# Block 2's spectrum by row number mod 4, its filter turned by transfers, and two product sums of block 3 by accumulating transfers, in a convolution and SwiGLU kernel

## The chip, the cores and the metric

One Trainium2 chip, one of its cores. The metric is the device time of one execution in microseconds (us), from the run before the change: 261.34 us, the median of three runs (261.23 to 261.5). Engines are called as the profile calls them: PE (TensorE, matmuls), PEld (its weight loads), DVE (VectorE), ACT (ScalarE), POOL (GpSimd) and SP (SyncE, which here only issues transfers). Each engine works through its own instructions in the order in which the program issues them.

## The reference

```python
x = A_q                                   # 2048 x 640, bf16
n = layernorm(x)
k_shift = causal 4-tap convolution of A_k, per channel (A_shift_k)
kv = k_shift * A_v
y  = causal long convolution of kv with A_ssm_k, per channel (by FFT of length 2 * 2048)
y  = y + kv * A_ssm_D
h  = x + n * y
u  = layernorm(h)
out = h + (silu(u @ w_gate) * (u @ w_up)) @ w_down     # 640 -> 1728 -> 640
```

(This is the reference in short, not its text.) The long convolution is what the change touches: each output row depends on all earlier rows of kv.

## The kernel before

**Tiles.** The 2048 rows are cut into four blocks of 512 (`BLK`). Within a block, row n lies on partition n // 4 as its row r = n mod 4, so a block is a tile of 128 partitions x 4 rows x 640 channels, 640 KB in bf16. Block j's output is the sum over i of the kv of block i convolved with pieces j - i and j - i - 1 of the filter. Each product is made in a spectrum of 512 odd frequencies, computed as matmuls with constant cosines and sines (`WF`; back with `WI`). A spectrum is a tile "S" of 128 x 2 x 4 x 640: two halves, each with two cosine and two sine rows of 640 channels, 1.25 MB.

**Stages of block j**, in the names that the program gives them: `g` turns the piece of the filter so that time lies on partitions; `G` is its spectrum; `h` (function `window`, or `window_of` in block 3) makes from G of this and the previous piece what is multiplied; `k` makes kv; `X` is kv's spectrum; `m0` to `mj` are the products X[i] * H[j-i] added up (`mac`); `n` is layernorm's statistics of x; `i` is the inverse with gate and addition of x; `t` normalises and turns h; `f` is the block's feed-forward part. The feed-forward part of block j-1 is written among the convolution stages of block j, so PE always has one of the two to do; that of block 3 (`f3`) comes alone at the end.

**The spectrum** (`transform`, from L381). "sub", the plain way, makes for each of four groups c of frequencies the sum of rows 0 and 2 (evicted doubled), then that of all rows (evicted as half 0): 32 matmuls of 128 x 320 columns and 8 evictions (L364 on ACT or L367 on DVE); half 1 is one DVE subtraction (L410). "four" uses a symmetry between rows of the same parity: for the even and the odd rows apart it makes two rows of sums and two of doubled parts, 16 matmuls and 8 evictions in all; DVE makes the rest by two `diffs` (L439, half a tile each), then 'hi4' (L443) for half 1 and 'lo4' for half 0. If the name is in `ADDLO`, which lists 'X2' already, lo4 is not a DVE instruction but an accumulating transfer (`add_into`, L278): POOL issues a DMA which adds a 640 KB tile into another one in SBUF. Before the change only X3, G3 and the inverses i2 and i3 go by four.

**The filter turned** (`g_turned`, L452). Normally, for each r, PE transposes five 128 x 128 pieces into PSUM (L471) and ACT or DVE evicts them (L473). A block in `GTURN` has instead one ACT copy of the whole tile into the order of rows (L457) and four DMA transposes of 160 KB, issued by SP (L461).

**The products** (`mac`, L703). After the first product of a block, each further one is four pairs on DVE: a product into a scratch tile (L746) and an addition or subtraction into the sum A (L747). For a pair listed in `ADDP` DVE makes the product alone (L741), and an accumulating transfer adds it (as for m11 before).

**The inverse** (`inverse`, L810): DVE first makes the difference and sum of the halves (L823, L826; the sum of block 2 by an accumulating transfer, `ADDINV`), then in "four" blocks the even rows' part (L843) and the odd rows' part (L858); PE makes row r from them (L878), DVE gates it (L892) and x is added (L905 or a transfer of POOL). The new h is normalised (L804 on DVE, L807 on ACT) and turned by PE (L926, evicted in L928) in block 0, and by DMA in the others.

**The feed-forward part**: groups of 256 columns; weights of a group are two loads of 320 KB (L959, issued by SP or POOL) into one slot of "big"; matmuls in L1022, evicted by ACT (L1014 with silu, L1012 plain), multiplied by DVE (L1016), then the down projection (L1110). Blocks 0 to 2 send their output by an accumulating transfer of POOL (L1117).

**What sets the order.** All instructions are first recorded as operations with their engine, tiles and dependencies (class `Plan`), and issued in an order written out by hand, the list `ORDER`. A negative number there stands for the operation's other engine: an eviction goes to DVE and not to ACT, a load to POOL's queue and not to SP's. Tiles take slots from small pools when their first operation comes in that order (12 of 640 KB called "big", 8 called "S", 5 rows, 4 pairs of PSUM banks) and give them back after their last; what comes next in a slot waits for it.

Of the kernel before, what the change touches and what calls it, by code (L numbers as in the profile page):

```python
# [41 lines left out]
LN1DVE = ()  # L42
LN2POOL = (1, 2)
HTURN = (1, 3, 2)
GTURN = (3,)
KTURN = (1, 2, 3)
SUM = {'X3': 'four', 'i2': 'four', 'i3': 'four', 'G3': 'four'}
ADDP = {(1, 1): ((0, 1),)}
ADDINV = (2,)
WHOLE3 = False  # L50
WARMUP = (18, 16, 16)
# [17 lines left out]
TW = PAD + BLK  # L69
CUTS = ("X0", "G0", "m", "i")  # L70
ORDER = [
# [36 lines left out]
SLOTS = {'S': 8, 'big': 12, 'kT': 0, 'tT': 1, 'row': 5, 'sg': 0, 'co': 2, 'ps': 4, 'sm': 6}  # L108
HOME = {t: "big" for t in ("scr", "x", "ld", "t4", "hT", "wgu", "diag")} | {"o": "row", "ps_c": "ps", "ps_f": "ps"}
SPLIT = ((0,), (1,))  # L110
# [102 lines left out]
def kernel(ctx: ExitStack, tc: tile.TileContext, A_q, A_k, A_v, A_shift_k, A_ssm_k, A_ssm_D, B_x,  # L213
# [19 lines left out]
    def new(tag):  # L233
        return Buf(HOME.get(tag, tag), None, tag)
# [26 lines left out]
    def dve(ns, fn, r, w, holds=()):  # L261
        return plan.add("dve", ns, fn, r, w, holds)
# [82 lines left out]
    def bits(halves=(0, 1), cs=(0, 1, 2, 3), ws=(0, 1)):  # L345

        return frozenset((h, c, w) for h in halves for c in cs for w in ws)
# [31 lines left out]
    def wide(n, ws):  # L379
        return n if len(ws) == 2 else n // 2 + 75  # L380
# [10 lines left out]
    def transform(src, dst, pieces, minus=None, name=None):  # L391

        how = SUM.get(name, "sub")
        for ws in pieces:
# [58 lines left out]
    def g_turned(g, drow=None):  # L453
        gT = new("t4")
        if plan.block in GTURN:
            by_r = new("scr")
# [356 lines left out]
    def inverse(A, x, n1, pieces=((0, 1),), minus=None, groups=(ROWS,)):  # L813
# [4 lines left out]
        for ws in pieces:  # L818
            if not minus:
# [10 lines left out]
                else:  # L830
                    dve(wide(1490, ws), low, [], [(A, bits(ws=ws))])
            four = not minus and SUM.get(f"i{plan.block}") == "four"
            if four:
# [404 lines left out]
    for j in range(1, NB):  # L1238
        def stage(name, j=j):
            plan.line(j, f"{name}{j}")  # L1240
# [23 lines left out]
        if last:  # L1264
            A = H[j]
            stage("m0")
            mac(A, X[0], H[j], True, at=(j, 0), adds=ADDP.get((j, 0), ()))
        stage("k")
# [4 lines left out]
        if not last:  # L1273
            stage("m0")
            A = Spec(new("S"))
            mac(A, X[0], H[j], True, at=(j, 0), adds=ADDP.get((j, 0), ()))
        for i in range(1, j + 1):
# [5 lines left out]
            else:  # L1283
                mac(A, X[i], H[j - i], False, adds=ADDP.get((j, i), ()), at=(j, i))
        stage("n")
# [45 lines left out]
```

## Time and profile before

| | |
|---|---|
| median of three runs | 261.34 us |
| the profiled execution | 261.3 us |
| its span | 259.6 us |
| granted clock of PE | 1.0 |
| PE busy | 251.3 us, 97% |
| DVE busy | 198.6 us, 77% |
| ACT busy | 180.0 us, 69% |
| POOL busy | 97.0 us, 37% |
| moved by DMA | 45.38 MB, 175 GB/s on average |

How to read it: the profile's page has numbered parts. The first gives the busy time of each engine, the second the same in 40 equal slices, a digit being tenths. Part 4 follows the chain of work that ended last back from the end. Part 5 groups instructions by line, engine, operation and tile: busy time, the mean of one, then the idle time before them with what ended it ("<- engine tile line"). Part 6 lists transfers with the median time from issue to landing. Beside the page there are views of the trace: the waits of one engine, its timeline with start, duration and idle time in brackets, and tables of busy time by stretch. In a timeline row "x4" is four instructions in a row that are shown as one. Matmuls are pipelined and their ends are modelled, so one is best priced from the start of a row to the start of the next. "Landing" counts from the issue of a transfer to its arrival. A busy share over the whole span mixes stages that have different limits; the stage shows which wait ends last there.

### The profile page before, as it was taken

To read this page: it belongs to the slowest core of one execution; us is meant where nothing else is said; L and a number is where in the kernel's file an instruction comes from. 1 tells how busy PE (TensorE), PEld (TensorE's weight loads), DVE (VectorE), ACT (ScalarE), POOL (GpSimd) and SP (SyncE) were. 2 spreads that over 40 slices of the span, in tenths; PEclk is the share of its full clock that TensorE was granted. 3 is DMA by queue.
4 is the path that set the end of the run, shared out by engine and by line. 5 is a ranking of instruction groups with operands and counts; after the bars stand their busy time and mean duration, and the time that the engine had idled before them with its cause. 6 is when DMAs were issued, how large, how long until landed. Compare 5 with 4: busy or idle time off the path is not lost.

```text
span 259.6 us, 4700 instructions
## 1 busy us (share of the span) xinstructions
PE 251.3 (97%) x1803; PEld 154.2 (59%) x1818; DVE 198.6 (77%) x259; ACT 180.0 (69%) x297; POOL 97.0 (37%) x115
## 2 busy tenths in 40 slices
PE   8999899999998999999999999999999999999994
PEld 7967577654654477754465477544456764444663
DVE  4679999999998999999999999999998200004403
ACT  2899999999998998569855985655497134637200
POOL 7961300008914199926117962240951022000000
PEclk9999999999999999999999999999999999999999
DMA  6997999979999998999997965994498546000002
GB/s 218 403 251 119 289 252 340 280 115 279 247 238 168 182 217 204 190 191 201 214 231 110 299 151 107 198 238 130 100 215 255 101 77 70 8 0 0 13 15 76
DMA packets 64752, 45.38 MB, mean 175 GB/s; under 512 B 31014, under 2 KB 60267, under 8 KB 64731
## 3 DMA queue, kind: packets, MB, share of 16 engines
q1 hardware_dynamic: 58896, 32.96, 51.1%
q0 software_dynamic: 5824, 12.13, 24.9%
q8 instruction: 14, 0.23, 0.4%
q14 instruction: 8, 0.06, 0.1%
q10 hardware_dynamic: 10, 0.01, 0.0%
HBM read 30.01 MB, written 4.59 MB: 133 GB/s over the span
## 4 chain that ended last, share of the span: by engine, by line
PE 78%; ACT 9%; DMA 6%; DVE 2%; issue 2%; SPq 1%; ACTq 0%; DVEq 0%
PE ps L1022 40%; PE ps L1110 23%; PE ps L375 10%; DMA big<-in_B_w_up_dram 4%; PE ps L878 3%; DMA big<-in_A_q_dram 3%; ACT T L565 2%; ACT big L364 1%; ACT S L364 1%; PE ps L648 1%; ACT row L757 1%; ACT big L664 1%; ACT big L473 1%; ACT tT L1014 1%; DVE row L892 1%
## 5 line engine op out<-in xcount | busy, mean ns | idle before, releaser
L1022 PE MATMUL ps<-big,big 128*128 128x512 bf16 x525 | 119.9, 379 | 1.7 <-DMA big<-in_B_w_up_dram 0.8
L1022 PEld LDWEIGHTS <-big 128*128 128x128 bf16 x540 | 52.5, 98 | 61.1 <-DMA big<-in_B_w_up_dram 1.3
L1110 PE MATMUL ps<-wd,tT 128*128 128x320 bf16 (+1 forms) x416 | 60.3, 299 | 0.0
L1110 PEld LDWEIGHTS <-tT 128*128 128x128 bf16 x416 | 40.7, 98 | 16.3
L1016 DVE TENSOR_TENSOR tT<-tT,co 128x2048 bf16<-128x2048 bf16 x12 | 14.5, 1219 | 34.4 <-ACT tT L1014 32.4
L375 PE MATMUL ps<-big,WF 128*128 128x320 bf16 x240 | 39.1, 299 | 1.3 <-ACT big L364 1.0
L1012 ACT CAST co<-ps 128x1024 bf16<-128x1024 f32 x24 | 24.2, 1011 | 17.3 <-PE ps L1022 16.8
L747 DVE TENSOR_TENSOR S<-S,big 128x2560 bf16<-128x2560 bf16 x23 | 34.3, 1492 | 1.2 <-DMA S<-big 0.5
L746 DVE TENSOR_TENSOR big<-S,S 128x2560 bf16<-128x2560 bf16 x23 | 34.1, 1485 | 0.2
L375 PEld LDWEIGHTS <-WF 128*128 128x128 bf16 x240 | 23.1, 97 | 12.8 <-issue 2.3
L1014 ACT ACTIVATE tT<-ps 128x1024 bf16<-128x1024 f32 x24 | 24.5, 1029 | 8.8 <-PE ps L1022 8.7
L757 ACT ACTIVATE row<-big 128x640 bf16<-128x640 bf16 x32 | 23.5, 742 | 1.8 <-DMA big<-in_A_q_dram 1.1
L807 ACT ACTIVATE row<-big,sm 128x640 bf16<-128x640 bf16 x23 | 20.3, 922 | 3.8 <-POOL sm L789 2.8
L1117 POOL DMA_DIRECT2D out_dram<-row x12 | 11.8, 1010 | 29.2 <-ACT row L1116 29.1
L364 ACT CAST S<-ps 128x320 bf16<-128x320 f32 (+1 forms) x36 | 19.4, 583 | 0.3
L1116 ACT CAST row<-ps 128x640 bf16<-128x640 f32 x12 | 8.1, 691 | 14.2 <-PE ps L1110 13.2
L364 ACT ACTIVATE big<-ps 128x640 bf16<-128x640 f32 (+1 forms) x24 | 15.6, 696 | 0.7 <-PE ps L375 0.7
L278 POOL DMA_DIRECT2D big<-row x8 | 7.0, 919 | 22.9 <-DVE row L892 22.9
L892 DVE SCALAR_TENSOR_TENSOR row<-row,ps 128x640 bf16<-128x640 bf16 x16 | 12.8, 815 | 1.1 <-PE ps L878 0.9
L278 POOL DMA_DIRECT2D S<-big x2 | 2.5, 1266 | 26.3 <-DVE S L719 19.1
L719 DVE TENSOR_TENSOR big<-S,S 128x2560 bf16<-128x2560 bf16 (+1 forms) x10 | 12.2, 1218 | 0.1
L959 POOL DMA_DIRECT2D big<-in_B_w_gate_dram x8 | 9.1, 1137 | 8.1 <-PE ps L1022 7.8
(110 smaller groups left out, 330.4 us busy)
## 6 DMA issues: line engine op xcount, KB each, us to landing
big<-in_B_w_up_dram SPq DMA_DIRECT2D x17, 320.0 KB, 5.1
big<-in_B_w_gate_dram SPq DMA_DIRECT2D x16, 320.0 KB, 4.7
big<-in_A_ssm_k_dram SPq DMA_DIRECT2D x4, 640.0 KB, 9.2
big<-in_A_q_dram SPq DMA_DIRECT2D x4, 640.0 KB, 7.6
big<-in_A_v_dram SPq DMA_DIRECT2D x4, 640.0 KB, 6.9
big<-in_B_w_gate_dram POOLq DMA_DIRECT2D x8, 320.0 KB, 7.2
big<-in_B_w_up_dram POOLq DMA_DIRECT2D x7, 320.0 KB, 6.7
wd<-in_B_w_down_dram SPq DMA_DIRECT2D x1, 2080.0 KB, 12.2
```

The costliest lines, as they stand in the source:

```text
L364: (lambda: nc.scalar.activation(dst(), src(), ACT.Copy, scale=2.0)) if twice else (lambda: nc.scalar.copy(dst(), src())),
L375: nc.tensor.matmul(ap(ps)[:, h, 0:NH], w, ap(src)[:, r, h * NH:(h + 1) * NH], start=(first and i == 0), stop=(last and i == len(rs) - 1), ...
L746: nc.vector.tensor_mul(flat2(b), X.part(xs), H.part(hs))
L747: f(A.part(dst), A.part(dst), flat2(b))
L757: act(825, lambda r=r, junk=junk: nc.scalar.activation(ap(junk), ap(x)[:, r, :], ACT.Square, scale=D ** -0.5, accum_out=sm(s, 1)[:, r:r + ...
L807: nc.scalar.activation(ap(row), ap(x)[:, r, :], ACT.Identity, bias=sm(s, 5)[:, r:r + 1], scale=sm(s, 4)[:, r:r + 1])
L892: nc.vector.scalar_tensor_tensor(two(ap(t)), two(ap(t)), 1.0, half(ap(ps)), op0=ALU.mult, op1=ALU.mult, accum_out=sm(s, 0)[:, r:r + 1])
L1012: act(1010, lambda ps=ps: nc.scalar.copy(ap(co)[:, at:at + 2, :], ap(ps)), src, [(co, gi % 2)])
L1014: act(1010, lambda ps=ps: nc.scalar.activation(ap(tT)[:, c:c + 2, :], ap(ps), ACT.Silu), src, [done(range(c, c + 2), ROWS)])
L1016: dve(1220, lambda: nc.vector.tensor_mul(ap(tT)[:, c - 2:c + 2, :], ap(tT)[:, c - 2:c + 2, :], ap(co)), [co], [done(range(c - 2, c + 2), R ...
L1022: nc.tensor.matmul(ap(ps)[:, i, :], ap(w)[:, k, off:off + P], ap(hT)[:, k, :], start=(k == 0), stop=(k == KT - 1))
L1110: nc.tensor.matmul(ap(ps)[:, hf, to:to + n], t, ap(wd)[:, c, col + (hf - hs[0]) * NH:col + (hf - hs[0]) * NH + n], start=(c == order[0]), ...
```

## The change

Four parts, all by settings and by the order:

- X2 is made the way of four (16 matmuls, two `diffs`, 'hi4', and 'lo4' by an accumulating transfer since 'X2' is in `ADDLO`).
- Block 2's g is turned by a copy of ACT and four DMA transposes.
- In block 3 the sum of X1's first product (the pair (0, 1) of m13) and the same one of m23 are added by accumulating transfers.
- The order is a new one. Besides the new operations it moves evictions between ACT and DVE, weight loads between POOL and SP (POOL issues 17 where it issued 20) and loads in the first 50 us; POOL has three accumulating transfers more and SP four transposes.

```diff
-GTURN = (3,)
+GTURN = (2, 3)
 KTURN = (1, 2, 3)
-SUM = {'X3': 'four', 'i2': 'four', 'i3': 'four', 'G3': 'four'}
-ADDP = {(1, 1): ((0, 1),)}
+SUM = {'X3': 'four', 'i2': 'four', 'i3': 'four', 'G3': 'four', 'X2': 'four'}
+ADDP = {(1, 1): ((0, 1),), (3, 1): ((0, 1),), (3, 2): ((0, 1),)}
...
 ORDER = [
-    0, 2, 31, 1, 4, 5, 7, 10, 6, 8, 16, 13, 12, 11, 22, 29, 26, 37, 27, 14, 3, 15, 23, 28, 42, -39, 9, 35, -37, 24, 39, 205, 40,
...
+    4, 0, 1, 42, 2, 31, 3, 16, 5, 7, 9, 6, 10, 13, 22, 29, 26, 14, 27, 39, 37, 15, -41, 28, 35, 38, 33, 12, 34, 41, 30, 8, 19,
...
```

The list has 914 operations before and 916 after. Each operation's number depends on how many were recorded ahead of it, so the two lists cannot be compared number by number. What the new order does to the stages named in the prediction: the first row of block 2's inverse that PE makes is an odd one; between X2's 'hi4' and m22's first product DVE has two pairs of m12 and two small products of f0; the slot freed by the last subtraction of block 3's window (L538) is given to the weights of the f1 group that stands right behind the first eight matmuls of i2; on POOL, i1's statistics stand ahead of X2's accumulating transfer.

70 rows, old and new, of the table ORDER are left out of this document.

## The prediction

> **What bounds the kernel now.** I read first the page: the busy shares, the 40 slices, the chain.
>
> ```profile
> PE 251.3 (97%) x1803; PEld 154.2 (59%) x1818; DVE 198.6 (77%) x259; ACT 180.0 (69%) x297; POOL 97.0 (37%) x115
> ...
> PE   8999899999998999999999999999999999999994
> ...
> DVE  4679999999998999999999999999998200004403
> ...
> PE 78%; ACT 9%; DMA 6%; DVE 2%; issue 2%; SPq 1%; ACTq 0%; DVEq 0%
> ```
>
> TensorE is busy 97% of the span and carries 78% of the chain; VectorE too is full from the fourth slice until shortly before the last stage. So an edit pays only what it takes off PE's row of work, minus the stalls that it puts in. The waits of PE are the second view.
>
> ```profile
> PE ps L375 <- ACT big L364: 1.0, 2, 0.8
> ...
> PE ps L1022 <- DMA big<-in_B_w_up_dram: 0.8, 1, 0.8
> ```
>
> PE loses about 2 us to others in the whole run; there is little to win there and much to lose. The sum below is made against the profiled execution, 261.3 us (span 259.6 us and 1.7 us around it); the median of the three runs is 261.34, the same within their scatter. About 0.2%, 0.5 us, is what a measurement of this kernel can tell from no change.
>
> **What leaves PE.** The timeline of PE gives two prices.
>
> ```profile
> 31.30 0.44 PE L471 MATMUL ps<-ident,big 128*128 128x128 bf16 x5
> 31.58 0.71 PE L375 MATMUL ps<-big,WF 128*128 128x320 bf16 x4
> ...
> 109.72 1.39 PE L375 MATMUL ps<-big,WF 128*128 128x320 bf16 x9
> 110.95 0.98 PE L1110 MATMUL ps<-wd,tT 128*128 128x320 bf16 x6
> ```
>
> Ends of matmuls are modelled, so I count from start to start: nine spectrum matmuls take 110.95 - 109.72 = 1.23 us, 0.137 each, and five transposes 0.28 us. X2 by row number mod 4 has 16 matmuls where it had 32: 16 x 0.137 = 2.2 us. Block 2's g is no longer turned by PE: 4 x 0.28 = 1.1 us. Together **-3.3 us** of a PE that is hardly idle, if all waits stay hidden.
>
> **What ACT takes on, and t0.** The copy ahead of block 3's transfers, and one of the evictions of turned g, show ACT's prices.
>
> ```profile
> 41.79 0.72 ACT L473 COPY big<-ps 128x640 bf16<-128x640 bf16 x1
> 42.38 1.93 ACT L364 ACTIVATE big<-ps 128x640 bf16<-128x640 f32 x3
> ...
> 77.61 2.55 ACT L457 COPY big<-big 128x2560 bf16<-128x2560 bf16 x1
> ```
>
> Turned by transfers, g2 costs ACT one copy of 2.55 us and saves it three evictions of 0.59 us start to start (41.79 to 42.38); the fourth was on DVE. The new order also shifts evictions and applications of the norm between ACT and DVE. With rows of this kind for each, ACT has 2.6 us more to do ahead of the last eviction of t0 (copy +2.55, g2 -1.77, evictions of g0 and G2 +2.36, X0, X1 and k1 +0.36, the norms of i0 and t0 -1.64, n1's first sum +0.73). That eviction is where block 0's convolution hands over to its feed-forward:
>
> ```profile
> 8.85 0.74 ACT L757 ACTIVATE row<-big 128x640 bf16<-128x640 bf16 x1 [1.07 <-DMA big<-in_A_q_dram]
> ...
> 48.23 1.41 ACT L928 COPY big<-ps 128x640 bf16<-128x640 bf16 x2
> ```
> ```profile
> ACT big L473 <- PE ps L471: 0.4, 1, 0.4
> ```
> ```profile
> 49.70 1.24 PE L1022 MATMUL ps<-big,big 128*128 128x512 bf16 x4
> ```
>
> ACT ends it at 49.64 and f0 begins at 49.70: a tie. Of the 2.6 us some 1.0 fits into two idle places of ACT before it (0.6 of the 1.07 us at 8.85, and the 0.4 us on L471), so t0 ends near 49.64 + 1.6 = 51.2. PE has 0.5 us more ahead of f0 (three more groups of G2 at 0.54, four sets of transposes less) and arrives near 50.2. I take a stall of **+1.0 us**; the bounds are 0 (all 2.6 us find idle places) and 2.1 (none does).
>
> **A stall that goes.** The 0.8 us on w_up was one weight load.
>
> ```profile
> 81.11 1.25 PE L1022 MATMUL ps<-big,big 128*128 128x512 bf16 x4 [0.78 <-DMA big<-in_B_w_up_dram]
> ```
>
>  In the new order other rows of block 1's inverse stand ahead of that group, and its load is issued earlier in SP's queue. I take **-0.8 us**; bounds -0.8 and 0.
>
> **What DVE gets and loses.** X2's two differences and its 'hi4' replace one subtraction; the timeline of DVE has the same three in block 3, then pairs of product and sum.
>
> ```profile
> 149.10 0.82 DVE L439 TENSOR_TENSOR S<-S 128x1280 bf16<-128x1280 bf16 x1
> 149.84 1.22 DVE L1016 TENSOR_TENSOR tT<-tT,co 128x2048 bf16<-128x2048 bf16 x1
> ...
> 156.83 0.42 DVE L1034 TENSOR_TENSOR tT<-tT,co 128x512 bf16<-128x512 bf16 x1
> 157.17 0.41 DVE L1039 TENSOR_TENSOR tail<-tail,co 64x512 bf16<-64x512 bf16 x1
> ...
> 158.70 1.49 DVE L443 TENSOR_TENSOR S<-S,big 128x2560 bf16<-128x2560 bf16 x1
> 160.11 1.49 DVE L746 TENSOR_TENSOR big<-S,S 128x2560 bf16<-128x2560 bf16 x1
> ...
> 163.04 1.48 DVE L746 TENSOR_TENSOR big<-S,S 128x2560 bf16<-128x2560 bf16 x1
> ```
>
> X2: 2 x 0.74 + 1.41 - 1.41 = +1.5 us. Blocks 3's products m13 and m23 each lose one sum, a pair of 2.93 us (160.11 to 163.04) becoming 1.41: -3.0 us. This is time in DVE's row and none in PE's, unless DVE is what PE waits for.
>
> **The new wait.** X2's low half, m13's and m23's sums come by accumulating transfers of 640 KB, issued by POOL. Four such transfers are in the trace; here are the issues and, from the DMA views around them, issue to landing.
>
> ```profile
> 59.46 1.28 POOL L278 DMA_DIRECT2D S<-big  x1 [19.05 <-DVE S L719]
> ```
> ```profile
> 160.77 1.25 POOL L278 DMA_DIRECT2D S<-big  x1 [7.26 <-issue]
> ```
> ```profile
> S<-big POOLq DMA_DIRECT2D x1, 640.0 KB, 9.9
> ...
> S<-S POOLq DMA_DIRECT2D x1, 640.0 KB, 9.9
> ```
> ```profile
> S<-big POOLq DMA_DIRECT2D x1, 640.0 KB, 6.8
> ```
> ```profile
> S<-S POOLq DMA_DIRECT2D x1, 640.0 KB, 7.7
> ```
> ```profile
> 69.43 1.49 DVE L747 TENSOR_TENSOR S<-S,big 128x2560 bf16<-128x2560 bf16 x1 [0.47 <-DMA S<-big]
> ```
>
> The range is 6.8 to 9.9 us, and the issue came 0.7 us after 'hi4' was through (158.70 + 1.41 = 160.11, issue 160.77). In the new order DVE has, between X2's 'hi4' and the first product of m22, which reads the summed half, only two pairs of m12 (2 x 2.93) and two small products of f0's tail (2 x 0.34): 6.5 us. So DVE, with all its queue behind it (m22, i2, block 3), waits 0.7 + 6.8 - 6.5 = 1.0 to 0.7 + 9.9 - 6.5 = 4.1 us. With 8.3 us, the middle of the four landings, it is **2.5 us**. POOL must also be free: i1's statistics stand just ahead of the add there.
>
> ```profile
> 100.63 0.93 POOL L1117 DMA_DIRECT2D out_dram<-row  x1
> ```
>
> They ended at the 100.6 us of this output, issued right behind them; 'hi4' I place near 100.7. No further delay, but no reserve. Behind the waiting add on POOL stand three of f0's outputs and one f1 load, with nothing near due.
>
> The row to set against it is the issue: 1.28 and 1.25 us beside a DVE that is busy throughout. The Trainium skill, "SBUF — State Buffer", section "SBUF: two separate sides", says that a transfer issued by GpSimd has its descriptors written by GpSimd through a port that a running DVE instruction may hold for its whole length. This trace agrees in so far as an issue costs POOL 1.25 to 1.28 us, but shows no issue beside an idle DVE; by that rule the landings of all three new adds lie at the long end, 9.9 us, and the sum would be 1.6 us higher than mine.
>
> **Does DVE's stall reach PE?** It does where block 2's inverse begins.
>
> ```profile
> 132.39 1.55 DVE L858 TENSOR_TENSOR S<-big 128x1280 bf16<-128x1280 bf16 x2
> ```
> ```profile
> 132.27 0.71 PE L878 MATMUL ps<-S,WI 128*128 128x320 bf16 x4
> ```
> ```profile
> DVE row L892 <- PE ps L878: 0.9, 2, 0.7
> ```
>
> PE begins with an odd row in the new order, which needs the last pair of L858. DVE had ended that at 133.9; it now has 0.9 us less ahead of it (a product of m03 and one of f1 later, X2 +1.5 and a differently shared eviction load), and two stalls of 0.5 (at 69.43, above) and 0.7 us go, since m11's gap grows from 8.7 to 11.2 us and i1's rows come in another order: 131.8 without the new wait. PE comes at 132.3 - 0.5 (work ahead) + 1.0 - 0.8 = 132.0. A tie, so nearly all of the 2.5 us goes to PE: I take **+2.4 us**, with bounds 0.8 and 3.9. If the two old stalls stay, it is 1.2 more; if the product sums slip further, less.
>
> **Block 3.** m13's add has 9.8 us before its reader, m23's 11.7, X3's 7.3 (it was 11.7): against 6.8 to 9.9 us from the issue this is up to 3.3 us of DVE at X3. But DVE has saved 3.0 us there, and PE, late by the stalls above, arrives later too; f3's start has hT3 ready several us ahead. I take 0; bounds 0 and +2.
>
> **g2's transfers.**
>
> ```profile
> DMA to landing us min/median/max: 5.6/5.7/7.6
> ```
>
> Block 3's four landed 5.6 to 7.6 us from issue. By SP's new order g2 can be loaded near 29, copied by ACT near 34 and landed by about 43, and G2 needs it near 46: I cost it at nothing. The cover is 3 us; without it PE would wait at G2, and f0's matmuls do not stand in front to fill the time.
>
> **The sum.** -3.3 + 1.0 - 0.8 + 2.4 = -0.7 us: 261.3 - 0.7 = **260.6 us**.
>
> **The rivals.** *All waits stay hidden:* X2's add lands in 6.8 us or less or the stall finds DVE ahead of PE, 261.3 - 3.3 + 1.0 - 0.8 = 258.2 us. For it speak the 6.8 of 160.77; against it the DMA share where X2's add will run, 0.99:
>
> ```profile
> 100.00:110.00 10.00, 10.00 (x76) 7.19 (x75) 9.80 (x8) 6.51 (x9) 9.53 (x10) 1.00 0.99 160
> ```
>
> (The last three columns are PE's clock, the DMA share and GB/s.)
>
> *Slower, by a weight load in i2.* The f1 group right behind i2's first eight matmuls gets the slot that the last subtraction of block 3's window frees, some 6.8 us ahead of its use. Landings of such loads differ by how full the queues are:
>
> ```profile
> big<-in_B_w_gate_dram SPq DMA_DIRECT2D x16, 320.0 KB, 4.7
> ```
> ```profile
> big<-in_B_w_up_dram POOLq DMA_DIRECT2D x1, 320.0 KB, 9.9
> ```
>
> 4.7 hides, 9.9 (between 118 and 135 us) is 3.1 us of PE idle, on top of my sum: 263.7 us. It decides from a landing of 6.8 + 1.2 = 8.0 us on, from where the time is above 261.8. For it: that window's own 9.9. Against it: a late DVE frees the slot and starts i2 equally late, and the page's median. *The change does not do what it says:* g2's transfers fall behind loads in SP's queue and G2 waits, 2 to 3 us: 263 us; the cover of 3 us speaks against it.
>
> **Chances.** My forecast 0.42 (259.1 with a landing of 6.8 us, 262.1 with 9.9); all hidden 0.20; weights late 0.28; g2 late 0.10. Faster by over 0.2%: 0.20 + 0.25 of the forecast's = 0.45. Within 0.2%: 0.13 of the forecast's and 0.05 of the weights' = 0.18. Slower: 0.04 + 0.23 + 0.10 = 0.37. The range of 8 in 10 goes from 258.2, the case of all hidden, to 263.9, a little over the weights' price; the bounds of the sum's own terms alone give 258.0 (-3.3 + 0 - 0.8 + 0.8) to 266.0 (-3.3 + 2.1 + 0 + 3.9 + 2.0), the far end only if all go wrong together.
>
> **What would show it.** Right: PE's matmul count down by 36, PE's busy time by 3 us; a DVE wait on a transfer into S ahead of m22 near 107 us, 1 to 4 us long; a PE wait on DVE at L878 near 132 us; a wait of about 1 us on L928 at f0's start. Wrong: no wait at m22 (then 258); a wait of PE on a w_gate or w_up load near 133 to 136 us (then 263 to 264); G2's matmuls waiting on a transfer near 46 us.

## The result and the profile after

| | before | after |
|---|---|---|
| median (six runs each) | 261.28 us | 265.06 us |
| ratio, 95% interval | | 1.0126 [1.0087, 1.0165] |
| profiled execution, span | 261.3, 259.6 us | 264.6, 262.9 us |

The changed kernel is slower by 1.3%; the two medians alone give a ratio of 1.014. (Disturbed runs, here one of the six, are left out of the ratios, not of the medians.) The profiled execution lies 0.5 us under its median. The page of after, parts 1, 2 and 4:

```profile
PE 248.9 (95%) x1768; PEld 150.8 (57%) x1782; DVE 197.7 (75%) x256; ACT 182.5 (69%) x297; POOL 97.3 (37%) x115
...
PE   8999879799999999979999899999999999999993
...
PE 72%; DMA 13%; ACT 9%; issue 2%; POOL 2%; DVE 1%; SPq 1%; ACTq 0%; POOLq 0%
```

PE has 2.4 us less work and still ends 3.3 us later. Its share of the chain fell from 78 to 72%, and that of DMA doubled. PE's slices are lower at the sixth and the eighth (33 to 39 and 46 to 53 us) and where f1 begins (the eighteenth). The waits of PE in after (total, times, longest) name what took PE's place:

```profile
PE ps L648 <- DMA T<-T: 1.5, 1, 1.5
PE ps L1022 <- DMA big<-row: 1.3, 1, 1.3
PE ps L375 <- ACT big L473: 1.1, 2, 0.9
PE ps L375 <- ACT S L364: 0.9, 2, 0.8
...
PE ps L1022 <- ACT co L1033: 0.7, 1, 0.7
PE ps L1110 <- DVE row L1127: 0.6, 1, 0.6
PE ps L926 <- ACT big L928: 0.6, 2, 0.5
```

None of these stood in the list of before above 0.2 us; its 0.8 us on w_up is gone. The two on L375, for evictions of ACT, lie ahead of f0. Where others stand is seen in PE's timeline of after:

```profile
37.93 2.72 PE L648 MATMUL ps<-pairs,T 128*128 128x64 bf16 x78 [1.47 <-DMA T<-T]
...
52.37 0.44 PE L926 MATMUL ps<-ident,row 128*128 128x128 bf16 x5 [0.48 <-ACT big L928]
...
53.73 1.24 PE L1022 MATMUL ps<-big,big 128*128 128x512 bf16 x4
...
115.49 10.95 PE L1022 MATMUL ps<-big,big 128*128 128x512 bf16 x49 [1.33 <-DMA big<-row]
```

The last two rows are the first matmuls of f0 and f1. These starts are the best ruler here. PE has 0.5 us more work ahead of f0 than before (12 spectrum matmuls more, 20 transposes less) and 3.3 us less from f1 on; a start that is later than that is stall:

| us | f0 | f1 | f2 | f3 | end |
|---|---|---|---|---|---|
| before | 49.70 | 113.66 | 165.01 | 211.53 | 259.6 |
| after | 53.73 | 115.49 | 167.64 | 214.17 | 262.9 |
| shift | +4.0 | +1.8 | +2.6 | +2.6 | +3.3 |
| change of the work ahead | +0.5 | -3.3 | -3.3 | -3.3 | -3.3 |
| stall added so far | 3.5 | 5.1 | 5.9 | 5.9 | 6.6 |

More than half of the added stall lies ahead of f0, three quarters ahead of f1. Behind f1, where i2 and the product sums of block 3 stand, 1.5 of the 6.6 us are added.

### The profile page after: what moved, and what is told of

Read it like the earlier page. It is cut to its first block, busy times and chain, and to the rows that moved or that the text cites. A ratio compares the mean times of both kernels' runs of the same rounds, so it can differ in the third digit from the quotient of the medians.

```text
span 262.9 us, 4650 instructions
## 1 busy us (share of the span) xinstructions
PE 248.9 (95%) x1768; PEld 150.8 (57%) x1782; DVE 197.7 (75%) x256; ACT 182.5 (69%) x297; POOL 97.3 (37%) x115
## 4 chain that ended last, share of the span: by engine, by line
PE 72%; DMA 13%; ACT 9%; issue 2%; POOL 2%; DVE 1%; SPq 1%; ACTq 0%; POOLq 0%
PE ps L1022 44%; PE ps L1110 19%; DMA big<-row 4%; DMA T<-T 4%; PE ps L878 4%; PE ps L648 3%; DMA big<-in_A_q_dram 3%; PE ps L375 2%; ACT big L364 2%; ACT row L757 2%; ACT S L364 2%; DMA wd<-in_B_w_down_dram 2%; ACT row L807 2%; POOL pairs L1185 1%; ACT row L796 1%
## 5 line engine op out<-in xcount | busy, mean ns | idle before, releaser
L1110 PE MATMUL ps<-wd,tT 128*128 128x320 bf16 (+2 forms) x416 | 60.6, 299 | 0.6 <-DVE row L1127 0.6
L1016 DVE TENSOR_TENSOR tT<-tT,co 128x2048 bf16<-128x2048 bf16 x12 | 14.6, 1219 | 36.9 <-ACT tT L1014 31.4
L375 PE MATMUL ps<-big,WF 128*128 128x320 bf16 x224 | 37.0, 298 | 3.4 <-ACT big L473 1.1
L746 DVE TENSOR_TENSOR big<-S,S 128x2560 bf16<-128x2560 bf16 x21 | 31.2, 1485 | 2.6 <-DMA S<-big 1.7
L747 DVE TENSOR_TENSOR S<-S,big 128x2560 bf16<-128x2560 bf16 x21 | 31.3, 1492 | 0.7
L375 PEld LDWEIGHTS <-WF 128*128 128x128 bf16 x224 | 21.7, 97 | 15.1 <-issue 5.6
L757 ACT ACTIVATE row<-big 128x640 bf16<-128x640 bf16 x32 | 23.6, 738 | 2.0 <-DVE big L905 2.0
L807 ACT ACTIVATE row<-big,sm 128x640 bf16<-128x640 bf16 x24 | 21.0, 915 | 2.1 <-DVE sm L789 1.1
L278 POOL DMA_DIRECT2D S<-big x5 | 6.3, 1280 | 19.7 <-DVE S L719 7.0
L796 ACT ACTIVATE row<-big 128x640 bf16<-128x640 bf16 x16 | 11.9, 742 | 2.2 <-DMA big<-row 1.7
L278 POOL DMA_DIRECT2D big<-row x8 | 8.4, 1393 | 12.2 <-ACT row L807 6.4
L1185 POOL TENSOR_SCALAR pairs<-row,taps 128x64 bf16<-128x64 bf16 x20 | 12.4, 647 | 0.1
L878 PEld LDWEIGHTS <-WI 128*128 128x128 bf16 x96 | 9.1, 98 | 5.8 <-DVE S L826 0.6
```

What stands on the lines that cost most here:

```text
L375: nc.tensor.matmul(ap(ps)[:, h, 0:NH], w, ap(src)[:, r, h * NH:(h + 1) * NH], start=(first and i == 0), stop=(last and i == len(rs) - 1), ...
L746: nc.vector.tensor_mul(flat2(b), X.part(xs), H.part(hs))
L747: f(A.part(dst), A.part(dst), flat2(b))
L757: act(825, lambda r=r, junk=junk: nc.scalar.activation(ap(junk), ap(x)[:, r, :], ACT.Square, scale=D ** -0.5, accum_out=sm(s, 1)[:, r:r + ...
L807: nc.scalar.activation(ap(row), ap(x)[:, r, :], ACT.Identity, bias=sm(s, 5)[:, r:r + 1], scale=sm(s, 4)[:, r:r + 1])
L878: nc.tensor.matmul(ap(ps)[:, w, 0:NH], m, src[:, w * NH:(w + 1) * NH], start=(i == 0), stop=(i == len(terms) - 1))
```

## The experiments

Medians are given with the ratio to before in the same call. Runs of kernels with the new order scatter by 0.8 to 4 us (before by 0.5 to 2 within a call, in the first by 3.3), and the median of before itself lay between 260.44 and 261.28 us from call to call, so differences among them of less than 2 us decide nothing. Numbers in diffs of `ORDER` are operations. In kernels built on the list of before, or with lines put in, lines of the profile are shifted by one to three.

**Order and operations apart.** All four edits in the order of before, each new operation where the one that it replaces stood:

```diff
 (before)
+GTURN = (2, 3)
+SUM = {'X3': 'four', 'i2': 'four', 'i3': 'four', 'G3': 'four', 'X2': 'four'}
+ADDP = {(1, 1): ((0, 1),), (3, 1): ((0, 1),), (3, 2): ((0, 1),)}
```

> All four edits with the order of before; the new operations stand where the ones they replace stood. Theory A (the loss is in the new order, chiefly around f0's start and f1's start): the start of f0 stays near 49.7 to 51 us, and the time is at or below that of before plus the wait for X2's add, whose reader here stands only one pair of DVE away (some 4 us): 259 to 264 us. Theory B (the edits load DVE's and the DMA queues' time and cost it themselves): 265 us or more, with f0's start late as well.

Measured 293.73 us, 1.128 [1.1251, 1.1309]. The waits of DVE and of PE in this kernel:

```profile
DVE big L747 <- DMA S<-big: 22.1, 3, 11.3
```
```profile
PE ps L1111 <- DVE tT L1017: 8.1, 1, 8.1
PE ps L879 <- DVE S L844: 6.6, 2, 6.3
```

Behind three accumulating transfers the next product on DVE waits for their landing, 22 us in all. And f0 begins at 55.85, against the expectation: the copy of g2 stands at 43.32 in ACT's queue here, an eviction behind it comes late, and the transposes come late too, as PE's timeline shows.

```profile
46.49 3.08 PE L376 MATMUL ps<-big,WF 128*128 128x320 bf16 x14 [2.72 <-ACT big L365]
51.18 0.69 PE L376 MATMUL ps<-big,WF 128*128 128x320 bf16 x2 [1.61 <-DMA big<-big]
```

So the edits cannot be had in the places of the operations that they replace, g2's among them. The counterpart, the new order with the operations of before:

```diff
 (after)
+GTURN = (3,)
+SUM = {'X3': 'four', 'i2': 'four', 'i3': 'four', 'G3': 'four'}
+ADDP = {(1, 1): ((0, 1),)}
```

> The new order with none of the edits: X2 by 32 matmuls, g2 turned by PE at the place of the copy, all product sums on DVE. Theory A: the start loss stays (f0's first matmul at 53 us or later) and 3.3 us of PE work come back: 266 to 269 us. Theory B: the loss goes with the edits: 261 to 263 us.

Measured 266.11 us, 1.0233 [1.0199, 1.0268]. **The order alone costs 2.3%, about 6 us.** The edits inside it give back 2.8 us by the ratios (1.0233 against 1.0126, from two calls) and 1.0 us by the medians, for 3.3 us of PE work. In its profiled execution the stall added so far is 3.6 us at f0, 2.8 at f1, 3.6 at f2, 4.1 at f3 and 4.5 at the end (span 264.1); in after it was 3.5, 5.1, 5.9, 5.9 and 6.6. So the stall at f0 belongs to the order, and in these two executions the edits add some 2 us between f0 and f1. This kernel has no copy of g2 on ACT, and f0 begins even later, by the 1.1 us of transposes that are back on PE:

```profile
54.95 1.24 PE L1022 MATMUL ps<-big,big 128*128 128x512 bf16 x5
```

So the late f0 does not need g2's transfers. It does not clear ACT of g2, though. All four evictions of g2 are on ACT in this order and take as long as the copy in after (2.56 us), as ACT's timeline shows:

```profile
36.41 2.51 ACT L473 COPY big<-ps 128x640 bf16<-128x640 bf16 x4 [3.81 <-PE ps L471]
```

**The two late starts.** One kernel gives PE two rows of i0 (with their gates, additions and a square sum) ahead of k1, whose transfer it waited for at 37.93; one puts the norm of the last h1 row ahead of f0's last outputs on ACT.

```diff
 (new_i0_rows_before_k1)
-173, 233, -235, 175,
+173, 161, 155, 233, -235, 175,
...
 (new_t1_row_before_outputs)
-474, 381, 390, 391, 473, 307, 306, 394,
+474, 307, 381, 390, 391, 473, 306, 308, 394,
...
```

> After, with the last two rows of block 0's inverse (PE, their gate and addition on DVE, one square sum on ACT) moved ahead of k1's matmuls. Theory A (i0's end is held by k1's matmuls, which wait for a transfer into T): t0 and f0 begin 1.5 to 3 us earlier and the time is 262 to 263.5 us. Rival (ACT, busy without a gap in the first 50 us, ends t0 late anyway): under 0.5 us of gain, 264.5 to 265.1 us.

> After, with t1's last row normalised on ACT ahead of the two evictions of f0's output (L1116), of which the second waited 1.45 us for a row slot, and its transpose issued with the others. Theory A: the 1.33 us that PE waits for that transpose at f1's start go: 263.3 to 264 us. Rival: DVE, which waits for X2's add meanwhile, or the tail of block 2 takes the place: 264.5 to 265.1 us.

Measured 266.48 us, 1.0227 [1.0184, 1.0269], with f0 at 55.18; and 267.14 us, 1.0228 [1.0177, 1.0278], f1 at 117.33 with a wait of 4.14 us on the same transposes. Neither repairs its start. The four transposes of h1 (L919, 95 to 125 us), issue to landing, in after and then in before:

```profile
DMA to landing us min/median/max: 4.5/6.9/7.2
```
```profile
DMA to landing us min/median/max: 4.0/4.8/4.9
```

In the kernel with the row moved forward they take up to 10.1 us. SP's own queue, after and then before (where the other two of h1 follow at 105.47):

```profile
95.32 6.44 SPq L461 DMA_TRANSPOSE big<-big  x3
101.88 8.52 SPq L919 DMA_TRANSPOSE big<-row  x4
```
```profile
80.19 6.33 SPq L461 DMA_TRANSPOSE big<-big  x4
...
101.55 3.19 SPq L919 DMA_TRANSPOSE big<-row  x2
```

In after, loads and block 3's transposes are issued right ahead of h1's; before, block 3's were over 15 us earlier. A late transpose also holds its row's slot, for which ACT's output eviction waits, with the last norm (L807) behind it in ACT's queue, as ACT's timeline of after shows:

```profile
106.42 0.69 ACT L1116 CAST row<-ps 128x640 bf16<-128x640 f32 x1 [1.45 <-DMA big<-row]
107.00 0.92 ACT L807 ACTIVATE row<-big,sm 128x640 bf16<-128x640 bf16 x1
```

**X2's low half, and k1's copies.** The accumulating transfer of X2 replaced by a DVE addition; and k1's two transfers put ahead of the POOL fill that they stand behind.

```diff
 (new_x2_low_half_on_dve)
-ADDLO = ('G1', 'G2', 'X1', 'X2', 'X3')
+ADDLO = ('G1', 'G2', 'X1', 'X3')
 (new_k1_copies_before_fill)
-99, 367, 17, 104,
+99, 367, -204, -203, 17, 104,
...
```

> After, with X2's low half added by DVE (1.4 us) and not by the accumulating transfer; all else as after. Theory C (the 640 KB add, issued at 102.7 us, is what makes h1's last transposes land 7.2 us after their issue and f1 start late): the 1.3 us wait at f1's start and DVE's 1.7 us at m22 go, 263.4 to 264.2 us. Rival (they queue behind g3's three transposes and the stores that SP issues just ahead of them): the wait at f1's start stays and the time is 264.6 us or more.

> After, with POOL issuing the two transfers into k1's T tile ahead of the last of its five fills of tap pairs, which ran 5.3 us there. Theory D (k1's matmuls, and ACT's and DVE's evictions of them, wait for these transfers, so t0 and f0 are late): they land 2.5 us earlier, the waits of PE (1.5), ACT (1.4) and DVE (1.5) go, and f0 starts at about 52.3 us: 263.5 to 264.1 us. Rival (the work ahead of t0 on ACT is the bound): f0 starts at 53.2 us or later, 264.5 us or more.

Measured 264.46 us, 1.0141 [1.0098, 1.0184]; and 265.35 us, 1.0144 [1.01, 1.0188]. In time, X2's add costs nothing that can be told from the scatter (0.6 us in the median). In the trace it shows: without it h1's four transposes land sooner, PE does not wait for them, and f1 begins at 113.97.

```profile
DMA to landing us min/median/max: 3.8/4.4/4.9
```

With k1's wait gone f0 still begins at 53.80: ACT now meets the next late thing, the load of g2.

```profile
35.20 2.53 ACT L457 COPY big<-big 128x2560 bf16<-128x2560 bf16 x1 [2.08 <-DMA big<-in_A_ssm_k_dram]
```

**The old start.** The order of before up to f0's first matmul, then that of after; g2 turned by PE, the other three edits in. A second kernel has X2's low half on DVE too.

```diff
 (before's ORDER up to f0, then after's)
+SUM = {'X3': 'four', 'i2': 'four', 'i3': 'four', 'G3': 'four', 'X2': 'four'}
+ADDP = {(1, 1): ((0, 1),), (3, 1): ((0, 1),), (3, 2): ((0, 1),)}
 (second kernel)
+ADDLO = ('G1', 'G2', 'X1', 'X3')
```

> The order of before up to f0's first matmul, g2 turned by PE as before, then the new order for all the rest; X2 by 16 matmuls with its accumulating transfer, m13 and m23 with theirs. Theory A, in its part on the start: f0 begins at 49.7 us, three groups of G2 (1.6 us) come after that and not ahead of it, and the rest runs as in after: about 262.6 us. Rival (what the start gains is lost again at h1's transposes, X2's add or in i2): 264 us or more.

> As the kernel with the start of before and the new rest, and X2's low half added by DVE. With theories A and C both right: about 261.3 us, the time of before. If only A: 262.6 us. If neither: 264 us or more.

Measured 265.64 us, 1.0176 [1.0136, 1.0216], and 264.15 us, 1.0118 [1.0092, 1.0144]. f0 begins on time, at 49.66 and 49.84. At f1 (115.89 and 113.62, where 2.2 us less work than before stands ahead) 4.4 and 2.2 us of stall have come again. Both have the wait that PE's timeline of the first shows:

```profile
76.36 1.30 PE L879 MATMUL ps<-big,WI 128*128 128x320 bf16 x8 [2.87 <-DVE big L824]
```

DVE reaches block 1's inverse at 74.81, as late as in after (74.41), where PE was late enough not to notice. In before it stood there at 70.96:

```profile
70.96 1.49 DVE L823 TENSOR_TENSOR big<-S 128x2560 bf16<-128x2560 bf16 x1
```
```profile
65.90 1.49 DVE L518 TENSOR_TENSOR S<-S,S 128x2560 bf16<-128x2560 bf16 x1
...
70.23 1.22 DVE L1016 TENSOR_TENSOR tT<-tT,co 128x2048 bf16<-128x2048 bf16 x1
...
74.41 1.49 DVE L823 TENSOR_TENSOR big<-S 128x2560 bf16<-128x2560 bf16 x1
```

The second fence is after: half of h2's window (L518) and f0's first product (L1016) now stand ahead of the inverse.

**The two small waits.** The square sum of i2 behind f1's tail copy (L1033), and f3's last rows in the order of before.

```diff
 (new_two_waits_mended)
-562, 513, 580, 582, 506,
+562, 580, 582, 513, 506,
...
-882, 896, 889, 876, 877, 884, 891, 886, 890, 892,
+882, 889, 876, 877, 884, 886, 890, 901, 902, 903,
 (new_all_mended: this, k1's copies first, X2's low half on DVE)
```

> After, with two places of the order mended that belong to none of the four edits: one square sum of block 2's inverse on ACT goes behind f1's L1033 copy (PE waited 0.68 us for it), and the last stores of f3 stand in the order of before (PE waited 0.65 us for L1127). If PE is what sets the end from f1's start on: 1.3 us less than after, 263.2 to 263.8 us. Rival (another engine is as late there): under 0.5 us less.

> After, with X2's low half on DVE, k1's copies issued ahead of the fill, and the two waits mended. If the waits add up: 264.5 (low half on DVE) - 1.3 - 0.5 = 262.2 to 263 us, still above the time of before, since the start of the new order stays late. If block 1's t1 and h1 set f1's start whatever else is mended: 263 us or more.

Measured 265.64 us, 1.0149 [1.0091, 1.0207], from 263.31 to 267.14; and 263.88 us, 1.0112 [1.0039, 1.0185]. Both small waits are gone from the traces, and the time is not: in the profiled execution of the first, its slowest, PE waits three times as long at f1.

```profile
PE ps L1022 <- DMA big<-row: 4.1, 1, 4.1
```

**Old order further; X2 alone.** The order of before up to X2's first matmul, with the mends; and the order of before throughout, with X2 by four as the only edit, its low half on DVE.

```diff
 (old_order_x2_by_four, on before)
+SUM = {'X3': 'four', 'i2': 'four', 'i3': 'four', 'G3': 'four', 'X2': 'four'}
+ADDLO = ('G1', 'G2', 'X1', 'X3')
```

> The order of before up to X2's first matmul (so through all of block 1's inverse, where the kernel with the start of before alone lost 2.9 us to DVE), g2 turned by PE; then the new order with the two waits mended; X2 by 16 matmuls, its low half on DVE, m13 and m23 with their transfers. Theory A (the order of the first 80 us is what costs, the edits gain PE's 2.2 us): 259 to 260.5 us, faster than before. Rival (the new rest needs the new start, DVE or ACT then sets f1's or f2's start): 261.5 us or more.

> The order of before with X2 by four alone, its low half on DVE. PE has 2.2 us less, DVE 2.9 us more ahead of i2. If DVE sets i2's start (its sums were ready only 1.2 us ahead of PE): PE waits about 3.9 us at L878 and the time is 262 to 263.5 us. If PE's work alone counts: 259.1 us.

Measured 272.25 us, 1.041 [1.0358, 1.0463], and 264.52 us, 1.014 [1.0085, 1.0195]. The first shows h1's late transposes (up to 8.3 us) at their costliest, in PE's timeline and in ACT's, in a kernel that has no X2 transfer at all:

```profile
113.81 1.22 PE L376 MATMUL ps<-big,WF 128*128 128x320 bf16 x4 [6.92 <-ACT row L1117]
```
```profile
113.07 0.69 ACT L1117 CAST row<-ps 128x640 bf16<-128x640 f32 x1 [8.38 <-DMA big<-row]
```

X2 by four, put where X2 stood and with its low half on DVE, is a loss by itself: 16 matmuls fewer, and f1 begins at 114.53 where it began at 113.66. DVE has 2.9 us more ahead of i2. Ahead of f1 PE waits 1.54 us for an output eviction of ACT, which waits 3.05 us for h1's transposes; these take 6.0 to 6.5 us here, though block 3's stand at 80 us as before and X2 has no transfer.

**What 16 matmuls are worth.** Before with half of X2's 32 matmuls left out, so that X2's spectrum is incomplete; nothing else differs.

```diff
     def forward(src, c, rs, ps, ws, first, last, holds, m=None):
+        if plan.name == "X2":
+            rs = rs[:1]
```

> Before, with 16 of X2's 32 matmuls left out (only the first of the two rows of each group is multiplied, so X2 is a wrong spectrum): nothing but 2.2 us of PE work goes, the order and all other engines stay. If PE's row of work sets the time, as the prediction had it: 258.3 to 259 us. If f1's start is set by the chain through DVE, ACT and h1's transposes: a gain under 1 us, 259.8 to 261 us, with a new idle time of PE between 100 and 115 us or in block 2's inverse.

Measured 259.90 us against 260.97, 0.9963 [0.993, 0.9996]: **1.0 us (by the interval 0.1 to 1.8) for 2.2 us of PE work**. f1 begins 0.7 us earlier, at 112.94, with all 2.2 us of work gone ahead of it. Part of the rest is seen as waits, as in this row, which was 1.0 us in before:

```profile
PE ps L378 <- ACT big L364: 1.5, 3, 0.8
```

**Block 3's transposes early; no product sums.** To clear SP ahead of h1, block 3's four transposes put right behind their copy; the same with all mends; and after without the two new product sums.

```diff
 (new_g3_turned_early; new_g3_early_all_mended with the mends besides)
-361, 609, 611, 619, 354,
+361, 609, 611, 619, 622, 623, 621, 620, 354,
 (new_no_product_adds)
-ADDP = {(1, 1): ((0, 1),), (3, 1): ((0, 1),), (3, 2): ((0, 1),)}
+ADDP = {(1, 1): ((0, 1),)}
```

> After, with g3's four transposes issued by SP directly behind the copy that they read (as before did, near 80 us) and not directly ahead of h1's. Theory E (they hold up h1's transposes in the queue): h1's last transpose lands within 5 us, f1's wait for it (1.3 us in the profile of after, 4.1 in two others) goes, 263 to 264 us, and the runs lie closer together. Rival (X2's transfer and the rest of the traffic is enough): 264.5 us or more.

> The same with X2's low half on DVE and the two waits mended. With theory E and the mended waits adding up: 261.5 to 262.5 us, near before but not under it, since f0's late start stays. If h1's transposes are late for another reason: 263.5 us or more.

> After, with m13's and m23's sums back on DVE (3.0 us more of DVE work in block 3, two transfers of 640 KB less). PE waited for nothing in block 3 in after, so if DVE has slack there: the same as after, 264.5 to 265.5 us. If DVE becomes late at i3: up to 2 us more, with PE waiting at L878 near 195 us.

Measured 273.01 us, 1.0411 [1.0336, 1.0487]; 270.94 us, 1.0364 [1.0332, 1.0396]; 266.01 us, 1.0181 [1.0128, 1.0235]. The first two don't test what they were made for: slots go by the order, and now a scratch tile of m02 got the slot that the transposes were reading. DVE's timeline of the first:

```profile
95.77 1.49 DVE L719 TENSOR_TENSOR big<-S,S 128x2560 bf16<-128x2560 bf16 x1 [7.98 <-DMA big<-big]
```

The third says that the product sums by transfer neither help nor hurt beyond the scatter (264.51 to 267.34).

**Block 1's inverse first.** On the old start with the low half on DVE and the mends, and on after alone: half of h2's window and f0's first product moved behind the subtraction of i1.

```diff
 (new_i1_first, on after)
-335, 324, 432, 271, 338,
+335, 324, 271, 338,
...
-326, 407, 347, 320,
+326, 407, 320,
...
+282, 432, 347, 348, 437,
```

> The kernel with the start of before, the new rest and X2's low half on DVE (264.2 us), with h2's second half and f0's first product on DVE moved behind i1's L823, and the two waits of the tail mended. Theory G (DVE's order ahead of L823 is the price of the new order once the start is on time): PE's wait of 2.9 us for L823 falls to 0.5 or less and 1.3 us of mended waits come off: 260 to 261.5 us. Rival (h1's transposes or evictions set f1's start anyway): 262.5 us or more.

> After, with only these two DVE instructions moved behind L823. PE reaches i1 late there, so by theory G nothing is gained at i1 and little in the end: 264.3 to 265.2 us. If DVE's chain through i1 and t1 to f1 is what sets f1's start whatever PE does: 262.5 to 263.5 us.

Measured 263.04 us, 1.007 [1.004, 1.01], and 267.75 us, 1.0229 [1.0173, 1.0285]. The first (g2 is turned by PE in it) is the fastest kernel with new operations, and still slower than before. Its wait moved on by one step, from the subtraction to the next DVE instruction of the same inverse:

```profile
73.80 1.26 PE L879 MATMUL ps<-big,WI 128*128 128x320 bf16 x8 [0.33 <-DVE big L824]
...
79.27 3.54 PE L879 MATMUL ps<-S,WI 128*128 128x320 bf16 x16 [2.05 <-DVE S L827]
```

## Why the prediction was wrong, step by step

| step | forecast | runs |
|---|---|---|
| PE's work (X2, g2) | -3.3 | count right (35 records fewer); worth 1 to 2.8 in the new order, and X2's 2.2 about 1.0 in the order of before |
| t0 and f0 on ACT | +1.0 (0 to 2.1) | 3.5 of stall |
| w_up | -0.8 | gone |
| X2's add at i2 | +2.4 | DVE waits 1.7; PE does not |
| block 3's sums | 0 | 0 within the scatter |
| g2's transfers | 0 | no wait of PE on them in after |
| order between f0 and the end | no term | 3.1 of added stall, 1.6 of it ahead of f1 |

**The step that failed first is "What ACT takes on, and t0".** It counted 2.6 us more for ACT ahead of t0's last eviction and let 1.0 of them fall into idle places that the order of before had. The count was near: from 8 us to the end of that eviction ACT is busy for 39.9 us in before and 42.0 in after. The handover was right too: the eviction ends near 53.5, and f0 begins at 53.73. But ACT's idle time did not shrink by 1.0 us, it grew from 1.7 to 3.5. In after it waits for DVE and for PE in two places where it did not before:

```profile
36.63 0.74 ACT L757 ACTIVATE row<-big 128x640 bf16<-128x640 bf16 x1 [1.24 <-DVE big L905]
...
39.44 1.29 ACT L664 CAST big<-ps 128x640 bf16<-128x640 f32 x2 [1.40 <-PE ps L648]
```

The second is k1: ACT waits for PE, and PE had waited for k1's transfer (37.93). f0 starts late in the new order without g2's transfers (54.95), and in the order of before with them in the old place (55.85); it is on time (49.66) with the whole old start and g2 turned by PE. So either is enough to delay it; in after the copy has an earlier place, and the order without it gives as much stall (3.6 us against 3.5).

POOL looks like one link: in after the fills of the shift's matrices run beside DVE's first products, and k1's transfers stand behind them. POOL in after, then in before:

```profile
12.12 1.95 POOL L1185 TENSOR_SCALAR pairs<-row,taps 128x64 bf16<-128x64 bf16 x4
...
21.43 5.26 POOL L1185 TENSOR_SCALAR pairs<-row,taps 128x64 bf16<-128x64 bf16 x4
26.50 1.51 POOL L563 DMA_DIRECT2D T<-T  x2
```
```profile
18.32 2.35 POOL L1185 TENSOR_SCALAR pairs<-row,taps 128x64 bf16<-128x64 bf16 x4
27.73 1.51 POOL L563 DMA_DIRECT2D T<-T  x2 [7.06 <-ACT big L473]
```

Four fills took 5.26 us there and 1.95 or 2.35 elsewhere. But k1's transfers are issued 1.2 us earlier in after than in before; what is longer is their landing, up to 10.6 us against 8.2. And moving them ahead of the fills moved f0 by 0.07 us only. No single wait holds f0: k1's transfers, the load of g2 and ACT's evictions all come late, close behind one another, and what one mend frees the next one takes.

**The second is the sum itself.** It charged the new order for three named places and held the rest to be as before. The order alone costs about 6 us. Behind f0, after loses 1.3 us at f1's start (4.1 in others), and 0.7 and 0.6 us at L1033 and L1127; the 3.4 us by which DVE comes later to i1 are hidden only as long as PE is late itself.

**"Does DVE's stall reach PE?"** was taken as a tie, with nearly all going to PE. The wait itself came as forecast, 1.7 us where the bounds were 1.0 and 4.1. DVE's and POOL's timelines of after:

```profile
110.39 1.49 DVE L746 TENSOR_TENSOR big<-S,S 128x2560 bf16<-128x2560 bf16 x1 [1.73 <-DMA S<-big]
```
```profile
102.71 1.30 POOL L278 DMA_DIRECT2D S<-big  x1 [3.50 <-DVE tT L1034]
```

The add landed 7.4 us after its issue, not at the 9.9 us of the slower reckoning. DVE was through L858 at 136.3, and PE came to i2 at 136.86, not at 132, and had no wait at L878 there. So this term came to nothing only because PE was late itself; DVE was ready 0.6 us ahead of it. What the add does cost PE was not in the sum: it is in flight from 102.7 to 110 us beside h1's transposes. Eight kernels with the order of after from f0 on and with this transfer have h1's last landing at 7.0 to 10.1 us, four without it at 4.4 to 5.0, and PE waits for these transposes at f1's first matmul (0.76 to 4.14 us) in six of the eight and in none of the four. (The two kernels with block 3's transposes turned early, 5.5 us with it and 2.6 without, are left aside.) In time the pairs differ by 0.6 us (after) and 1.5 us (old start) in the median, less than the scatter.

The rivals failed too: no weight load held i2, PE had no wait on g2's transfers, and "all waits hidden" held at i2 and not elsewhere; the kernel is slower, but by neither of the two causes that were named for that. The median lies 1.2 us above the range's upper end. It lies inside the far bounds of the sum's terms (258.0 to 266.0), but that is chance: the stall at f0 went past its bound of 2.1, the one at i2 stayed out, and 3.1 us had no term.

**What stays open.** Why h1's transposes take from 2.6 to 10.1 us. X2's transfer has a part in it, as above, and is not all: kernels without it reach 6.5 us (X2 by four in the order of before) and 8.3 us (the one of 272.25 us). In both of these block 3's transposes stand at 80 us, so these are not needed either. Where the four landed in 2.6 us each (block 3's turned early, all mends), the DMA share from 106 to 116 us was 0.40, against 1.14 in after; so the load of the DMA engines is the likeliest cause, which is argued and not shown. From execution to execution this wait is also the first suspect for the scatter of the new order; only profiled executions show it. Nor does any run take ACT's load of g2 out of the new order, so what of f0's stall is due to it is open.

## What to carry to other kernels

Where one engine is 97% busy and every handover is close to a tie, price a new order as an edit of its own: run the old operations in it, and read the start of each stage against the work counted ahead of it. Idle places of the old order are no cover in a new one. PE work taken away was worth about half its size in the old order. A transfer that frees an engine is still in flight beside others: read the landing of those too. Mending one wait after another helps little when several sources are late by the same few us; the next one is then waiting already.

## What the runs showed of the hardware

**PE's clock can fall after idle times of 2 to 3 us, and need not.** The windows of the kernel with the old start, around its wait of 2.87 us (PE's clock is the third column from the end):

```profile
74.00:76.00 2.00, 0.00 (x0) 0.00 (x0) 1.97 (x2) 2.00 (x4) 0.00 (x0) 1.00 0.65 196
76.00:78.00 2.00, 1.64 (x10) 1.06 (x11) 2.00 (x4) 2.00 (x5) 0.00 (x0) 0.86 1.11 287
78.00:80.00 2.00, 2.00 (x7) 0.78 (x6) 2.00 (x3) 0.42 (x1) 0.00 (x0) 0.50 2.03 150
80.00:82.00 2.00, 2.00 (x14) 1.25 (x13) 0.88 (x3) 0.00 (x0) 0.00 (x0) 0.78 0.68 106
```

The clock is 0.50 from 78 to 80 us, after the wait is over, and short of full in the windows beside it: (0.14 + 0.50 + 0.22) x 2 = 1.7 us of a full clock's work are lost on top of the wait. The sister kernel with X2's low half on DVE has a wait of 2.87 us at the same place, and its clock stays at 1.00:

```profile
78.00:80.00 2.00, 2.00 (x15) 1.23 (x13) 2.00 (x4) 0.60 (x1) 0.00 (x0) 1.00 1.12 193
```

From the end of the wait to the next group of f0 the same matmuls take 7.12 us in the first (76.36 to 83.48) and 5.43 in the second (76.55 to 81.98): the 1.7 us again. So the length of the wait alone does not decide. Of the ten waits of PE between 2.0 and 3.1 us in the traces here eight were followed by a clock of 0.50 to 0.54 in some window of 2 us and two (2.87 and 2.90) by none; the five of 4.05 to 8.13 us by 0.50; after the 1.33 and 1.47 us of after the clock stayed at 1.00. The Trainium skill, "TensorE: Matmul & The Clock Gate", section "Part 1: The HAM clock gate", gives half the clock after at least one idle window of about 3.4 us, and the full one again after about as long a busy time. The depth, 0.50, agrees; here a wait of 2.01 to 3.02 us was enough in eight cases of ten.

**GpSimd beside VectorE.** The four fills of 5.26 us ran beside DVE products of 0.82 us each with both inputs in SBUF, end to end from 19.8 us on, as DVE's row in after shows:

```profile
22.05 0.81 DVE L719 TENSOR_TENSOR big<-S,S 128x1280 bf16<-128x1280 bf16 x1
```

Each fill took 1.3 us there on average, 0.44 in the median of all 20: it is longer by about the length of one such product. The Trainium skill, "SBUF — State Buffer", section "SBUF: two separate sides", says that DVE with two SBUF inputs and a GpSimd instruction that reads SBUF exclude each other for a whole instruction; the 0.9 us more for each fill agrees with that. An accumulating transfer's issue, 1.30 us at 102.71, costs as much as before.
